# Dealing the mixing in two parts of nine steps per pair of heads, and scoring tiles 3 and 4 last

## The chip, the cores and the metric

The kernel runs on one core of a Trainium2 chip. The metric is device time in microseconds of one execution; the median of three runs of the kernel before is 802.76 us (802.55 to 803.49).

## What is computed

A windowed causal attention with a linear distance bias, for 8 batches of 8 heads, 576 positions and 64 channels a head; its output, as 576 rows of 512 channels per batch, goes through a gated mixing over the positions and a channel layer.

```python
scores = scale * np.matmul(q, k.transpose(0, 1, 3, 2))
mask = (rel >= 0) & (rel < window)                 # window = 128
scores = np.where(mask, scores + bias[None], -1000000000.0)
attn = np.exp(scores - np.max(scores, axis=-1, keepdims=True))
attn = attn / (np.sum(attn, axis=-1, keepdims=True) + 1e-09)
x = np.matmul(attn, v)                             # then heads side by side
theta = x @ w_theta
y = einsum('ts,bsd->btd', w_tok_r, x * cos(theta)) + einsum('ts,bsd->btd', w_tok_i, x * sin(theta))
u = x + y
out = u + np.maximum(u @ w_ch, 0.0)
```

## The kernel before

Queries are cut into five tiles (`TILES`, four of 128 and one of 64), and each meets a window of up to 256 keys. Products that need more than one pass of precision are made of a high and a low part (`qh`, `ql`, `kh`, `kl`, and so on), three products for one.

Four kinds of work make up a batch:

- **Attention**, by pairs of heads, four pairs a batch (`attend`). `Pair.scores(tiles)` (L272) makes the scores of some tiles for both heads of a pair: per tile six products with a contraction over 64 rows, two at a time, one for each head (L289, `s_ps`), then a DVE instruction that adds the bias and finds the row's extreme (L296), then an exponential on ACT (L300). The calls are (0, 2), (3, 4) and (1,), and belong to the *next* pair, one pair ahead. `flip` (in `turned`, L320) transposes a head's weights into `t_ps`; ACT copies them to fp16 (L366), DVE makes the low part (L367); `values` (L337) multiplies them with the values into `acc`, 27 products a head; `finish` (L343 to L346) scales and writes `x_sb`.
- **Turning** (`turn`): the batch's `x_sb` is transposed (L390), multiplied with `w_theta` (L410), and its sine and cosine are taken on ACT (L431, L432) and multiplied in (DVE, and L381, L382 for the split into `z_hi` and `z_lo`).
- **Mixing** (`mix`): 8 groups of 27 products (L469), each group in its own PSUM tile `mm`. One *step* of the generator is three products, so a group has nine steps and a batch 72. A group ends with L474 (DVE), L475 (ACT), L476 (POOL).
- **Channels** (`channels`, L489): 8 groups of 12 products, then L492 and an output DMA (L494).

While a batch is mixed, the next batch's attention runs: `attend` draws steps of the mixing (`other`) between its own calls. The sine and the exponential need different tables on ACT, so the exponentials of the scores are held behind the batch's last sine (`behind`).

The written order is not the order on the engines. The framework's scheduler orders the instructions on each engine by a priority that follows the written order, and by when it reckons each one ready; mixing, channels and turning carry an offset on that priority (`MIX`, `CHAN`, `ROTATE`). So a step that is written in one place can stand somewhere else on PE.

Other names: `prepare` (L175 to L234) splits a pair's q and k and issues the load of the next pair (DMAs from SP, L176, L178); `measure` (L201) is a DVE reduction over a group of four heads of values `vb`, which a DMA (L192) brings; `spread_scales` (L209 to L221) turns its result into scales; `ready` (L248 to L250) splits a head's values.

Of the kernel before, what the change touches and what calls it, by code (L numbers as in the profile page):

```python
# [29 lines left out]
DEPTH = 1  # L30
# [16 lines left out]
def attn_moe_kernel(ctx: ExitStack, tc: tile.TileContext, qt, kt, vx, wth, wtok, wch, band, out):  # L47
# [125 lines left out]
    def load_pair(p):  # L173
        b, h = divmod(2 * p, H)
        qr = ld.tile([128, S], F32, name="qr")  # L175
        nc.sync.dma_start(out=qr, in_=qt[b, h:h + 2].rearrange("h d s -> (h d) s"))  # L176
        kr = ld.tile([128, S], F32, name="kr")
        nc.sync.dma_start(out=kr, in_=kt[b, h:h + 2].rearrange("h d s -> (h d) s"))  # L178
        return qr, kr
# [15 lines left out]
    def measure(g):  # L195

        vb = group_v[g]
        most = rings["most"].take()  # L200
        nc.vector.tensor_reduce(out=most, in_=vb[:, :, :, :64], axis=mybir.AxisListType.XY, op=ALU.max,  # L201
                                apply_absolute_value=True)
        nc.vector.tensor_scalar(out=most, in0=most, scalar1=2.0 ** -100, scalar2=None, op0=ALU.max)
        group_v[g] = vb, most
# [20 lines left out]
    def split_pair(p, raw):  # L225

        qr, kr = raw
        qh, ql, kh, kl = (qk.tile([128, S], F32R, name=name) for name in ("qh", "ql", "kh", "kl"))
        sc = scales[:, p % (H // 2):p % (H // 2) + 1]
        nc.scalar.activation(qh, qr, AF.Copy, scale=sc)  # L230
        nc.vector.scalar_tensor_tensor(out=ql, in0=qr, scalar=sc, in1=qh.bitcast(F32), op0=ALU.mult,  # L231
                                       op1=ALU.subtract)
        nc.scalar.copy(kh, kr)  # L233
        nc.gpsimd.tensor_tensor(out=kl, in0=kr, in1=kh.bitcast(F32), op=ALU.subtract)  # L234
        return (qh, kh), (ql, kh), (qh, kl)
# [265 lines left out]
    def prepare(p):  # L501

        if 0 <= p - 1 < pairs and p - 1 not in parts:
            parts[p - 1] = split_pair(p - 1, raw.pop(p - 1))
        if p < pairs and p not in raw:
            raw[p] = load_pair(p)

    def step(stream, k=1):
        for _ in range(k):
            next(stream, None)  # L510
# [11 lines left out]
    def attend(b, x_sb, other, first, behind):  # L522

        for g in range(H // 2):
            p = b * H // 2 + g
            one, two = first.pop(0).heads
            new = None
            if p + DEPTH < pairs:
                new = Pair(p + DEPTH)
                first.append(new)  # L530

            def scores(tiles):
                if new is not None:
                    new.scores(tiles, behind)

            one.flip(0)
            one.flip(1)
            scores((0, 2))
            step(other, 6)
            one.values(0)  # L540
            one.values(1)
            one.finish(x_sb)
            if new is not None:
                new.heads[0].ready()
            two.flip(0)
            two.flip(1)
            scores((3, 4))
            if p % 2 == 0 and p + 2 < pairs:
                measure(p // 2 + 1)
            step(other, 6)  # L550
            two.values(0)
            two.values(1)
            two.finish(x_sb)
            scores((1,))
            if p % 2 == 0 and p + 2 < pairs:
                spread_scales(p // 2 + 1)
            prepare(p + DEPTH + 2)
            if new is not None:
                new.heads[1].ready()
            step(other, 6)  # L560

    def start(x_sb, load):

# [48 lines left out]
    def ahead(prods, chans):  # L612

        for k, _ in enumerate(prods):
            if k in AHEAD:
                next(chans)
            yield

    def ahead0(prods, chans):

        rest = urgent(unpack(LATE, ((uf, "xtf"),)), LATE0)
        for k, _ in enumerate(prods):
            if k % 4 == 3:
                next(rest, None)
            yield
        yield from rest
        for _ in range(AHEAD0):
            next(chans)
            yield
# [25 lines left out]
    for b in range(B):  # L655
        chans = urgent(channels(b, st[b]), CHAN if b else CHAN0)
        mixing = urgent(mix(st[b]), MIX if b else MIX0)
        other = ahead(mixing, chans) if b else ahead0(mixing, chans)
        if b + 1 < B:
            x_sb = xp.tile([128, NT, DM], F32, name="x_sb")  # L660
            attend(b + 1, x_sb, other, first, st[b]["sin"])
        for _ in other:
            pass
        if b + 1 < B:
            if first:
                st[b + 1]["exp"] = first[-1].exp
            rotated(urgent(turn(x_sb, st[b + 1]), ROTATE), chans)
        for _ in chans:
            pass
# [47 lines left out]
```

## Time and profile before

| what | value |
|---|---|
| median of the runs | 802.76 us |
| the profiled execution's own time | 803.77 us |
| its span, first to last instruction | 802.0 us |
| granted TensorE clock, mean | 0.991 |
| DVE busy | 567.2 us (71%) |
| ACT busy | 481.8 us (60%) |
| POOL busy | 260.6 us (32%) |

The span has a start (weights are loaded and split, attention of batch 0, to about 105 us), a turn of batch 0 (to about 155 us), seven stages in which batch b is mixed while batch b+1 is attended and then turned, and a tail in which the last batch is mixed alone. Five of the seven stages repeat with a period near 86.8 us. Busy time of PE includes matmuls that overlap, so it is read with the starts of the instructions, which the timeline gives.

### The profile page before, as it was taken

How to read it: one execution, taken by the hardware profiler on the slowest of the kernel's cores; microseconds unless marked ns; L12 is line 12 of the kernel's file. 1: busy time of each engine (PE TensorE's matmuls, PEld its weight loads, DVE VectorE, ACT ScalarE, POOL GpSimd, SP SyncE). 2: the span in 40 equal slices, each digit the busy share in tenths (PEclk: the TensorE clock that was granted, in tenths of full speed). 3: DMA queues.
4: the chain of work that ended last, by engine and by line, in shares of the span. 5: the costliest groups of instructions: out<-in, count | busy, mean ns of one | idle time of the engine just before them, and what ended most of it. 6: DMA issues, size and time to landing. Idle time of an engine off the chain costs nothing.

```text
span 802.0 us, 16393 instructions
## 1 busy us (share of the span) xinstructions
PE 740.5 (92%) x6338; PEld 656.0 (82%) x6338; DVE 567.2 (71%) x1535; ACT 481.8 (60%) x962; POOL 260.6 (32%) x324
## 2 busy tenths in 40 slices
PE   3565996889999999999999999999999999999998
PEld 2454875778788898889889988999888988899897
DVE  6997449877866877677767786687858776664712
ACT  5544347576567656775667657865767566844610
POOL 3576005552232322432252214232333225210530
PEclk9999999799999999999999999999999999999999
DMA  6541121132110221022112212023102211000001
GB/s 236 173 152 60 34 90 42 42 90 65 45 60 22 72 87 53 31 65 64 55 62 68 65 45 60 23 67 99 45 30 65 64 57 64 2 1 31 30 1 60
DMA packets 29549, 49.65 MB, mean 62 GB/s; under 512 B 2592, under 2 KB 19104, under 8 KB 29472
## 3 DMA queue, kind: packets, MB, share of 16 engines
q1 hardware_dynamic: 29472, 48.61, 19.3%
q8 instruction: 50, 0.82, 0.4%
q14 instruction: 27, 0.22, 0.1%
HBM read 39.16 MB, written 9.44 MB: 61 GB/s over the span
## 4 chain that ended last, share of the span: by engine, by line
PE 60%; DVE 16%; ACT 15%; issue 4%; DMA 3%; POOL 1%; SPq 0%; ACTq 0%; DVEq 0%; POOLq 0%
PE mm L469 19%; PE mm L489 10%; PE mm L410 8%; PE t_ps L320 8%; PE s_ps L289 7%; PE acc L337 7%; ACT s_sb L300 5%; DVE f L425 2%; DVE s_sb L296 2%; ACT z_hi L381 2%; ACT g L431 2%; PE mm L390 2%; DVE pt L367 1%; DMA vb<-in_vx_dram 1%; ACT L431 1%
## 5 line engine op out<-in xcount | busy, mean ns | idle before, releaser
L469 PE MATMUL mm<-wtk_hi,z_hi 128*128 128x288 f32 x576 | 172.8, 305 | 0.3 <-DVE xtf L474 0.3
L469 PE MATMUL mm<-wtk_lo,z_hi 128*128 128x288 f32 x576 | 172.0, 303 | 0.0
L469 PE MATMUL mm<-wtk_hi,z_lo 128*128 128x288 f32 x576 | 167.4, 301 | 0.0
L300 ACT ACTIVATE s_sb<-s_sb,fixed 128x256 f32<-128x256 f32 (+2 forms) x320 | 128.2, 465 | 56.5 <-DVE fixed L296 56.4
L296 DVE CUSTOM_DVE_ANT_0 s_sb<-s_ps,fixed 128x256 f32<-128x256 f32 (+2 forms) x320 | 105.5, 375 | 26.3 <-PE t_ps L320 12.7
L320 PE MATMUL t_ps<-fixed,s_sb 128*128 128x128 f32 (+1 forms) x576 | 104.0, 295 | 9.9 <-ACT s_sb L300 8.3
L469 PEld LDWEIGHTS mm<-wtk_hi,z_hi 128*128 128x128 f32 x576 | 108.8, 190 | 3.4 <-DVE xtf L474 0.5
L469 PEld LDWEIGHTS mm<-wtk_lo,z_hi 128*128 128x128 f32 x576 | 109.0, 190 | 2.0
L469 PEld LDWEIGHTS mm<-wtk_hi,z_lo 128*128 128x128 f32 x576 | 107.3, 190 | 0.9
L476 POOL TENSOR_TENSOR u_lo<-xtf,u_hi 128x288 fp32r<-128x288 f32 x64 | 52.6, 828 | 139.5 <-ACT u_hi L475 131.8
L367 DVE SCALAR_TENSOR_TENSOR pt<-t_ps,pt 128x512 f16<-128x512 f32 x112 | 74.8, 683 | 24.1 <-ACT pt L366 24.1
L382 POOL TENSOR_TENSOR z_lo<-g,z_hi 128x512 fp32r<-128x512 f32 x40 | 55.3, 1382 | 111.5 <-ACT z_hi L381 111.5
L320 PEld LDWEIGHTS t_ps<-fixed,s_sb 128*128 128x128 f32 (+1 forms) x576 | 67.4, 150 | 27.5 <-ACT s_sb L300 12.3
L289 PE MATMUL s_ps<-kh,qh 64*128 64x256 f32 (+2 forms) x320 | 57.5, 343 | 26.8 <-DVE fixed L296 19.8
L366 ACT ACTIVATE pt<-t_ps 128x512 f16<-128x512 f32 x112 | 63.3, 594 | 24.4 <-PE t_ps L320 23.9
L234 POOL TENSOR_TENSOR kl<-kr,kh 128x576 fp32r<-128x576 f32 x32 | 46.9, 1465 | 74.1 <-ACT kh L233 64.7
L289 PEld LDWEIGHTS s_ps<-kh,qh 64*128 64x128 f32 (+1 forms) x320 | 33.1, 192 | 41.7 <-DVE fixed L296 19.1
L337 PE MATMUL acc<-vh,pt 128*128 128x65 f16 x1008 | 61.2, 195 | 2.9 <-DVE pt L367 1.7
L337 PEld LDWEIGHTS <-pt 128*128 128x128 f16 x1512 | 52.8, 98 | 10.1 <-DVE pt L367 2.9
L289 PE MATMUL s_ps<-kh,ql 64*128 64x256 f32 (+2 forms) x320 | 50.8, 302 | 5.8 <-DVE ql L231 5.8
L337 PE MATMUL acc<-vl,pt 128*128 128x64 f16 x504 | 55.8, 193 | 0.0
L475 ACT CAST u_hi<-xtf 128x288 fp32r<-128x288 f32 x64 | 27.0, 430 | 44.5 <-DVE xtf L474 44.5
(111 smaller groups left out, 1570.0 us busy)
## 6 DMA issues: line engine op xcount, KB each, us to landing
vb<-in_vx_dram SPq DMA_DIRECT2D x16, 650.0 KB, 4.2
qr<-in_qt_dram SPq DMA_DIRECT2D x32, 288.0 KB, 3.1
kr<-in_kt_dram SPq DMA_DIRECT2D x32, 288.0 KB, 2.8
out_dram<-xtf SPq DMA_DIRECT2D x64, 144.0 KB, 1.8
xtf<-in_wtok_dram SPq DMA_DIRECT2D x4, 576.0 KB, 5.7
xtf<-in_wch_dram SPq DMA_DIRECT2D x4, 512.0 KB, 3.9
u_hi<-in_wtok_dram SPq DMA_DIRECT2D x3, 576.0 KB, 3.9
u_lo<-in_wtok_dram SPq DMA_DIRECT2D x2, 576.0 KB, 4.3
```

The costliest lines, as they stand in the source:

```text
L289: nc.tensor.matmul(ps[:qn, e, 256 * k:256 * k + kn], qm[rows, q0:q0 + qn], km[rows, k0:k0 + kn], start=(j == 0), stop=(j == len(self.terms ...
L296: nc.vector.tensor_tensor_reduce(out=sb, in0=ps[:qn, e, 256 * k:256 * k + kn], in1=bnd[:qn, c0:c0 + kn], scale=2.0 ** -((2 * self.p + e) % ...
L300: self.exp = nc.scalar.activation(sb, sb, AF.Exp, bias=least, scale=-1.0)
L320: nc.tensor.transpose(t_ps[:, off:off + w], self.sc[i][:, 128 * j:128 * j + 128], ident[:w, :w])
L337: nc.tensor.matmul(av[:, i, :r.shape[-1]], l, r, start=(n == 0), stop=(n == len(prods) - 1))
L366: nc.scalar.activation(pt[:, 0], t_ps, AF.Copy, scale=2.0 ** PEXP)
L367: nc.vector.scalar_tensor_tensor(out=pt[:, 1], in0=t_ps, scalar=2.0 ** PEXP, in1=pt[:, 0], op0=ALU.mult, op1=ALU.subtract)
L382: nc.gpsimd.tensor_tensor(out=z_lo[:, c, :], in0=z, in1=z_hi[:, c, :].bitcast(F32), op=ALU.subtract)
L410: nc.tensor.matmul(t_ps, a[:, c * 128:c * 128 + 128], w[:, c, :], start=(k == 0 and c == 0), stop=(k == len(prods) - 1 and c == 3))
L469: nc.tensor.matmul(y_ps[:, :HALF], z[:, c, m * 128:m * 128 + 128], w[:, c, cs], start=(k == 0), stop=(k == 26))
L476: nc.gpsimd.tensor_tensor(out=u_lo[:, m, cs], in0=xtf[:, m, cs], in1=u_hi[:, m, cs].bitcast(F32), op=ALU.subtract)
L489: nc.tensor.matmul(o_ps[:, :HALF], w[:, c, e * 128:e * 128 + 128], u[:, c, cs], start=(k == 0), stop=(k == 11))
```

## The change

Per pair of heads, the mixing was drawn in three parts of six steps; now it is drawn in two parts of nine, which is one group of 27 products each. The scores of tile 1 come before those of tiles 3 and 4 instead of after them, the second head's flips come ahead of them and of `ready` of the first head, `prepare` comes earlier (ahead of the scores of tiles 3 and 4), and the part of the mixing that closed the pair's turn is gone.

```diff
             scores((0, 2))
-            step(other, 6)
+            step(other, 9)
             one.values(0)
             one.values(1)
             one.finish(x_sb)
+            two.flip(0)
+            two.flip(1)
+            scores((1,))
             if new is not None:
                 new.heads[0].ready()
-            two.flip(0)
-            two.flip(1)
-            scores((3, 4))
             if p % 2 == 0 and p + 2 < pairs:
                 measure(p // 2 + 1)
-            step(other, 6)
+            prepare(p + DEPTH + 2)
+            scores((3, 4))
+            step(other, 9)
             two.values(0)
             two.values(1)
             two.finish(x_sb)
-            scores((1,))
             if p % 2 == 0 and p + 2 < pairs:
                 spread_scales(p // 2 + 1)
-            prepare(p + DEPTH + 2)
             if new is not None:
                 new.heads[1].ready()
-            step(other, 6)
```

The scheduler's order moves with it on every engine. On PE, before, in a stage of the repeating kind where the next pair's tiles 0 and 2 are scored among the mixing, these rows stand together (`s_ps` holds scores, `mm` a mixing group):

```order
L469 MATMUL mm<-wtk_hi,z_hi 128x288
L289 MATMUL s_ps<-kh,ql 64x192 x2
L289 MATMUL s_ps<-kl,qh 64x192 x2
L289 MATMUL s_ps<-kh,qh 128x256 x2
L289 MATMUL s_ps<-kh,ql 128x256 x2
L289 MATMUL s_ps<-kl,qh 128x256 x2
L469 MATMUL mm<-wtk_lo,z_hi 128x288
```

On PE now, in every second stage of the repeating kind, where tiles 0 and 2 are first scored among the mixing, the rows are (`acc` is the output of a head, `pt` its turned weights):

```order
L289 MATMUL s_ps<-kh,qh 64x192 x2
L289 MATMUL s_ps<-kh,ql 64x192 x2
L289 MATMUL s_ps<-kl,qh 64x192
L469 MATMUL mm<-wtk_hi,z_lo 128x288 x3
L337 LDWEIGHTS pt
L337 MATMUL acc<-vh,pt 128x65
L337 LDWEIGHTS pt
L337 MATMUL acc<-vl,pt 128x64
L289 MATMUL s_ps<-kl,qh 64x192
L289 MATMUL s_ps<-kh,qh 128x256 x2
L289 MATMUL s_ps<-kh,ql 128x256
```

The twelve score products are cut into more runs, with mixing and value products between them, and two of the cuts fall between the two heads of a pair of products (the rows without "x2").

On DVE, before, ahead of the first `measure` (L201) of a stage of the repeating kind, after the `vl` that last reads the old values:

```order
L250 SCALAR_TENSOR_TENSOR vl<-vb,fixed,vh 128x320
L367 SCALAR_TENSOR_TENSOR pt<-t_ps,pt 128x512 x2
L296 ISA s_sb_4134,fixed<-s_ps,fixed 128x128
L296 ISA fixed 128x1
L296 ISA s_sb_4135,fixed<-s_ps,fixed 128x128
L296 ISA fixed 128x1
L474 TENSOR_TENSOR xtf<-mm,xtf 128x288 x3
L231 SCALAR_TENSOR_TENSOR ql<-qr,fixed,qh 128x576
L201 TENSOR_REDUCE fixed<-vb 128x4
```

On DVE now, at the same place:

```order
L250 SCALAR_TENSOR_TENSOR vl<-vb,fixed,vh 128x320
L367 SCALAR_TENSOR_TENSOR pt<-t_ps,pt 128x512 x2
L474 TENSOR_TENSOR xtf<-mm,xtf 128x288 x3
L201 TENSOR_REDUCE fixed<-vb 128x4
L343 TENSOR_SCALAR fixed<-acc,fixed 128x5
L250 SCALAR_TENSOR_TENSOR vl<-vb,fixed,vh 128x320
L203 TENSOR_SCALAR fixed<-fixed 128x4
L367 SCALAR_TENSOR_TENSOR pt<-t_ps,pt 128x512
```

The two L296 and the `ql` no longer stand between the release of the old values and the reduction over the new ones.

## Prediction

> **What bounds the kernel now.** I began with the page, for the share of each engine and the slices.
>
> ```profile
> span 802.0 us, 16393 instructions
> PE 740.5 (92%) x6338; PEld 656.0 (82%) x6338; DVE 567.2 (71%) x1535; ACT 481.8 (60%) x962; POOL 260.6 (32%) x324
> PE   3565996889999999999999999999999999999998
> PEclk9999999799999999999999999999999999999999
> PE 60%; DVE 16%; ACT 15%; issue 4%; DMA 3%; POOL 1%; SPq 0%; ACTq 0%; DVEq 0%; POOLq 0%
> ```
>
> PE is busy nearly everywhere after the sixth slice, at full clock. The chain that ended last lies on PE for 60% of the span; DVE and ACT hold 31%, so they still decide some pieces. Then the windows, by stage: columns are length, busy time of PE, PEld, DVE, ACT and POOL with counts, granted clock, DMA share and GB/s.
>
> ```profile
> 105.00:155.00 50.00, 40.06 (x244) 32.40 (x244) 39.54 (x90) 29.18 (x53) 20.91 (x18) 0.93 0.23 69
> 155.00:249.70 94.70, 88.03 (x792) 78.17 (x793) 71.50 (x192) 61.06 (x122) 31.42 (x41) 0.96 0.19 59
> 423.60:510.40 86.80, 86.25 (x805) 77.10 (x804) 64.65 (x187) 58.07 (x117) 26.24 (x37) 1.00 0.19 58
> 683.90:756.20 72.30, 71.20 (x641) 64.36 (x640) 43.15 (x114) 44.01 (x91) 18.00 (x23) 1.00 0.04 13
> ```
>
> The row in the middle, 423.60:510.40, stands for the five stages that repeat. PE idles 86.80 - 86.25 = 0.55 us there: no engine's wait is left worth removing, and the number of products doesn't change. What can still change is how long PE takes for them, since their order changes. The first mixing stage is different: PE idles 94.70 - 88.03 = 6.67 us, waiting mostly for DVE (its waits come below).
>
> **What a score run costs PE.** The third view is PE's timeline in the repeating stage. The first column is the start; I read starts alone, since the ends of matmuls are modelled.
>
> ```profile
> 439.21 0.29 PE L469 MATMUL mm<-wtk_hi,z_lo 128*128 128x288 f32 x1
> 439.34 0.29 PE L469 MATMUL mm<-wtk_hi,z_hi 128*128 128x288 f32 x1
> 439.57 0.30 PE L289 MATMUL s_ps<-kh,ql 64*64 64x192 f32 x2
> 439.71 0.26 PE L289 MATMUL s_ps<-kl,qh 64*64 64x192 f32 x2
> 439.79 0.31 PE L289 MATMUL s_ps<-kh,qh 64*128 64x256 f32 x2
> 439.94 0.28 PE L289 MATMUL s_ps<-kh,ql 64*128 64x256 f32 x2
> 440.05 0.28 PE L289 MATMUL s_ps<-kl,qh 64*128 64x256 f32 x2
> 440.27 0.40 PE L469 MATMUL mm<-wtk_lo,z_hi 128*128 128x288 f32 x1
> 440.51 0.29 PE L469 MATMUL mm<-wtk_hi,z_lo 128*128 128x288 f32 x1
> ...
> 442.58 0.30 PE L469 MATMUL mm<-wtk_hi,z_hi 128*128 128x288 f32 x1
> 442.72 0.60 PE L320 MATMUL t_ps<-fixed,s_sb 128*128 128x128 f32 x4
> 443.07 0.38 PE L469 MATMUL mm<-wtk_lo,z_hi 128*128 128x288 f32 x1
> 443.29 0.29 PE L469 MATMUL mm<-wtk_hi,z_lo 128*128 128x288 f32 x1
> ```
>
> Mixing products follow each other every 0.13 us (439.21 to 439.34), and pairs of score products every 0.08 to 0.15 us, 0.12 in the mean. From the mixing product at 439.34 to the second one behind the scores, at 440.51, is 1.17 us. Two mixing products (0.26) and five pairs (0.60) make 0.86, so the run of scores has cost **0.31 us** beyond its products: 0.23 instead of 0.13 on entering, 0.22 and 0.24 on leaving. Full-height transposes don't: 442.58 to 443.29 is 0.71 us, and two mixing products and four transposes at some 0.11 are 0.70. So it is the change between 64-row and 128-row products that costs, whatever the number of products in a run.
>
> **The change part by part.** *Score runs.* I counted in PE's order how often score products stand in a run, with other work on both sides: 133 runs in the whole program before, 158 now. By stage of mixing, from the first: 16, 15, 17, 17, 17, 17, 8 before and 18, 19, 23, 21, 23, 21, 7 now; the start and the tail don't change. That is 25 more, at 0.31 us each 7.75 us. The bounds for one run are 0 (it lies where PE would have waited) and 0.40, nearly what a run costs when its product and weight loads also arrive late; I take 0.31, the row. The two extra runs of the first mixing stage I count as nothing, 0.62 less, since PE waits 6.67 us there anyway. Left: **+7.1**.
>
> *Pairs cut in two.* Some of the new cuts fall between the two heads' products of a pair, as in the second piece of the order. I count 25 of them beyond the few of before. Two products that start together take one spacing of 0.12; apart, each could take its own. Bounds 0 and 25 x 0.12 = 3.0; the rows show no cut pair, so I take the middle less a little, **+1.2**.
>
> The Trainium skill (TensorE: Matmul & The Clock Gate, Part 3: Packing small matmuls) says that products in different row groups start some 4 ns apart and run at once, but that products start and end in program order; by that a cut pair would lose the whole overlap, an estimate of 3.0 rather than 1.2 and a sum higher by 1.8. The rows of "x2" above agree with the overlap; what a cut pair costs no row quoted here shows.
>
> *Mixing steps.* The same 216 products stand in the stage, and "whole groups" isn't what PE gets: the order now has runs of mixing up to 42 products long and still cuts groups at 24, because the mixing's priority lets it fill in. A cut beside transposes costs nothing (the row at 442.72), so: 0.
>
> *The wait for the low part of `pt`.* The one wait of PE over 0.2 us in the repeating stage, from PE's timeline, and behind it rows of the chain of waits and of the groups by line in that stage:
>
> ```profile
> 433.34 0.20 PE L337 MATMUL acc<-vl,pt 128*128 128x64 f16 x1
> 433.76 0.24 PE L337 MATMUL acc<-vh,pt 128*128 128x65 f16 x2 [0.23 <-DVE pt L367]
> ...
> 423.62 1.28 ACT L300
> 424.91 5.12 ACT s_sb L300 x14
> ...
> L367 DVE SCALAR_TENSOR_TENSOR pt<-t_ps,pt 128x512 f16<-128x512 f32 x16 | 10.8, 684 | 3.4 <-ACT pt L366 3.4
> L366 ACT ACTIVATE pt<-t_ps 128x512 f16<-128x512 f32 x16 | 9.1, 595 | 3.6 <-PE t_ps L320 3.6
> ```
>
> The value products wait from 433.34 to 433.76 (0.42, instead of some 0.03), because ACT first had 14 held exponentials behind the table load, 1.28 + 5.12 us. Now 15 or 16 stand there, 0.4 to 0.8 us more; but PE has 5 to 6 us of work between these transposes and their value products, where it had 3.6. So this wait goes: -0.39 in each of five stages, **-2.0**. What is late next: later in the stage there are value products that follow their transposes after only 1.4 to 1.7 us of PE work, where the shortest before was 2.7 (the products that stand between in PE's order, each at its spacing in the timeline). ACT's copy and DVE's low part take 0.595 + 0.684 = 1.28 in a row, so 1.4 is just enough with empty queues and not enough with a score reduction ahead. Bounds per stage 0 and 2; I take 0.4, near the 0.39 of the row: **+2.0**.
>
> *`measure` and the values' DMA.* In the second piece of the order, DVE's reduction moves ahead, past two L296 and a `ql`. The transfer sets when it can start (rows of the waits, of the tile `vb`, and of DVE's timeline):
>
> ```profile
> DVE fixed L201 <- DMA vb<-in_vx_dram: 1.4, 1, 1.4
> DMA to landing us min/median/max: 4.1/4.1/4.2
> 436.52 1.49 DVE L201 TENSOR_REDUCE fixed<-vb 128x4 f32<-128x1280 f32 x1
> 435.74 0.85 DVE L231 SCALAR_TENSOR_TENSOR ql<-qr,fixed,qh 128x576 fp32r<-128x576 f32 x1
> 434.22 0.28 DVE L296 CUSTOM_DVE_ANT_0 s_sb<-s_ps,fixed 128x128 f32<-128x128 f32 x1
> ```
>
> The first reduction starts at 436.52 with DVE busy until then; without 0.85 and twice 0.21 (the spacing of the two L296 is below their 0.28) it is reached 1.2 us earlier, while the 4.1 us of the transfer don't shrink. DVE then stands for about that, and behind it in its queue are `finish`, a `vl`, and the low part that the next head's value products wait for. PE has some 24 to 30 mixing products (at 0.13, over 3 us) to do meanwhile, so I cost it at 0; if that cover were gone it is 1.2 a stage, six stages, 7 us.
>
> *`prepare` earlier.* Its q and k loads on SP pass the values' load and some output DMAs, and its `kl` on POOL stands ahead of a split of z. Before, SP's loads of k wait for buffers, not PE for loads:
>
> ```profile
> SPq L178 <- POOL kl L234: 194.2, 24, 15.9
> ```
>
> This is 194 us of waiting in 24 issues that nobody waited for; one `kl` ahead of the last `z_lo` could cost a POOL instruction, but ACT's exponentials stand in front of that z anyway. 0, with bounds -1 and +1.5 a stage at one place.
>
> *First mixing stage.* Here PE waits for DVE:
>
> ```profile
> PE s_ps L289 <- DVE fixed L296: 5.8, 3, 2.8
> PE mm L216 <- DVE fixed L213: 1.5, 1, 1.5
> ```
>
> The new order has one more score group ahead of the second of these waits, and six mixing products in front of the first score group behind it; both fill waiting, 0.5 us or so each: **-1.0**, with bounds -5 and +3, as DVE's work is the same and only its order moves.
>
> **The sum.** 7.1 + 1.2 - 2.0 + 2.0 - 1.0 = **+7.3 us**. The profiled execution took 803.77 us, so 811.1; the median of the runs is 1.0 below it, and on that scale the forecast is **810.1 us**.
>
> **The rivals.**
>
> *Faster, by the first stages.* If the new runs lie mostly where PE would otherwise wait, a run costs a tenth of a us, 2.5 in all, and a DVE order that lets PE through takes 5 of the 6.67 us of the first mixing stage and the 2.0 of the `pt` waits: 2.5 - 5 - 2.0 = -4.5, 798.3 us. It decides from the point where the stage 155 to 250 shrinks by more than the repeating stages grow. For it: only there is idle time to win, and PE's waits for score reductions before 172 us alone were 5.8 us. Against it: 0.55 us of idle time a repeating stage can't hide four to six new runs (1.2 to 1.9 us). Chance 0.18.
>
> *Nothing comes of it.* The runs are hidden or the scheduler has traded them for waits of the same size; the sum is between -1.6 and +1.6, 802.8. That the groups of 27 don't stand whole on PE speaks for it, the count of runs against it. Chance 0.14.
>
> *Waits take the stage.* The close value products wait a full score reduction and a low part more, twice a stage, 2 x 0.7 to 2 x 1.0, and `measure` stops DVE without cover: some 8 us on top, 818 us. Against it: DVE idles a quarter of the stage (64.65 of 86.80 busy). Chance 0.14.
>
> **How the numbers follow.** My forecast, more runs of scores with about the same waits, has 0.54. Slower by over 0.2% (1.6 us, what a measurement here can tell from no change) is the forecast and the waits, 0.68; same 0.14; faster 0.18. The range 800 to 817 leaves out the better part of the faster rival and the far side of the waits, some 0.2.
>
> **What would show it.** In the changed kernel's windows the repeating stages should come out 0.8 to 2 us longer each, in pairs of two kinds (the order alternates), with PE still idle under 1.5 us; the stage before 250 us should be equal or up to 1.5 us shorter. PE's timeline at the second piece of the order should show an extra 0.2 to 0.3 us at each cut. The wait at the first value products behind the exponentials should be gone. I am wrong if the repeating stages keep 86.8 us with 21 or 23 runs of scores, or if PE's idle time grows by more than the runs cost.

## The result, and the profile after

The changed kernel takes 820.72 us (median of 4 runs, 819.51 to 821.96), against 803.12 us (802.55 to 803.89) for the kernel before on the same chip: a ratio of 1.0219, 95% interval 1.0200 to 1.0237, or **+17.6 us**. The forecast was 810.1 us in a range of 800 to 817. The sign was right, and the size was not: it is more than twice what the sum gave, and outside the range.

First the page of the changed kernel, the lines that answer to those of before:

```profile
span 817.7 us, 16414 instructions
PE 754.9 (92%) x6338; PEld 660.3 (81%) x6338; DVE 570.4 (70%) x1535; ACT 483.1 (59%) x962; POOL 263.7 (32%) x324
PE   3566997799999999999999999999999999999998
PE 63%; DVE 20%; ACT 10%; issue 4%; DMA 2%; POOL 1%; SPq 0%; DVEq 0%; ACTq 0%; POOLq 0%
```

As many matmuls as before, 14.4 us more PE time and 3.2 us more DVE time. The share of DVE on the chain that ended last rose from 16% to 20%, while ACT's fell. That is the first hint that more than PE's order is at stake, and it says nothing of the place.

The place comes from cutting a stage at ACT's table loads. From the load of the exponential's table to the load of the sine's, the stage is mostly attention and mixing; from the sine's to the exponential's it is the turn. These are the windows of two stages of the kernel before (length, busy time of PE, PEld, DVE, ACT and POOL with counts, clock, DMA share, GB/s):

```profile
336.80:399.00 62.20, 61.10 (x637) 54.65 (x636) 47.16 (x153) 41.39 (x90) 14.29 (x29) 1.00 0.19 56
399.00:423.60 24.60, 24.51 (x165) 21.72 (x164) 17.45 (x35) 16.70 (x28) 11.93 (x9) 1.00 0.19 60
423.60:485.80 62.20, 61.73 (x642) 55.38 (x641) 47.22 (x153) 41.41 (x90) 14.35 (x29) 1.00 0.19 57
485.80:510.40 24.60, 24.51 (x165) 21.73 (x164) 17.43 (x35) 16.66 (x28) 11.89 (x9) 1.00 0.20 61
```

And the same two stages of the changed kernel:

```profile
337.20:399.80 62.60, 61.94 (x625) 54.49 (x623) 43.07 (x140) 39.57 (x86) 11.97 (x27) 1.00 0.20 58
399.80:428.60 28.80, 27.70 (x183) 23.51 (x183) 22.22 (x48) 19.07 (x32) 14.44 (x10) 1.00 0.17 49
428.60:491.20 62.60, 61.66 (x628) 54.63 (x627) 43.05 (x140) 39.20 (x85) 12.44 (x27) 1.00 0.19 57
491.20:518.80 27.60, 26.60 (x175) 22.70 (x174) 23.16 (x47) 18.92 (x33) 14.92 (x10) 1.00 0.16 50
```

A stage, an attention part and the turn behind it, went from 86.8 us to 91.4 and 90.2 us, and nearly all of it lies in the turn: 24.6 us became 28.8 and 27.6. Over the five repeating stages, cut in the same way, it is 19.3 us, all but 1.7 of it in the turns. DVE has 12 to 13 instructions and about 5 us more in the turn, and 4 us less in the attention; 10 to 18 matmuls moved the same way. The attention part lost that work and did not get shorter: 62.2 became 62.6 us. PE now idles 1.0 to 1.1 us in a turn, where it idled 0.1.

What PE waits for in the repeating stages is the next view, the table of PE's waits (total us, times, longest), first of the kernel before and then of the changed one:

```profile
PE acc L337 <- DVE pt L367: 1.4, 5, 0.5
PE t_ps L320 <- ACT s_sb L300: 1.1, 3, 0.4
PE mm L489 <- ACT xtf L403: 0.8, 4, 0.2
```

```profile
PE s_ps L289 <- DVE ql L231: 4.8, 5, 1.4
PE t_ps L320 <- ACT s_sb L300: 2.9, 6, 0.7
PE mm L410 <- DVE f L425: 0.9, 2, 0.4
```

The wait of the value products for `pt` is gone, as forecast. In its place stands one wait in each of the five stages for **`ql`**, the low part of q that `prepare` makes on DVE. PE's timeline shows one of them, in a turn of the changed kernel (start, length, and in brackets the idle time and what ended it):

```profile
496.91 0.30 PE L289 MATMUL s_ps<-kh,qh 64*64 64x192 f32 x2
498.21 0.31 PE L289 MATMUL s_ps<-kh,ql 64*64 64x192 f32 x2 [1.00 <-DVE ql L231]
498.36 0.26 PE L289 MATMUL s_ps<-kl,qh 64*64 64x192 f32 x2
```

PE has issued the products with `qh`, reaches those with `ql`, and stops 1 us in the middle of a score group. DVE's timeline at that place shows why `ql` is late:

```profile
494.94 1.47 DVE L436 TENSOR_TENSOR f<-x_sb,f 128x512 f32<-128x512 f32 x1
496.32 1.84 DVE L231 SCALAR_TENSOR_TENSOR ql<-qr,fixed,qh 128x576 fp32r<-128x576 f32 x1
498.08 0.68 DVE L425 SCALAR_TENSOR_TENSOR f<-f,mm 128x512 f32<-128x512 f32 x1
```

and POOL's, beside it:

```profile
494.42 1.43 POOL L234 TENSOR_TENSOR kl<-kr,kh 128x576 fp32r<-128x576 f32 x1 [8.34 <-ACT kh L233]
495.81 1.73 POOL L382 TENSOR_TENSOR z_lo<-g,z_hi 128x512 fp32r<-128x512 f32 x1
497.51 1.79 POOL L382 TENSOR_TENSOR z_lo<-f,z_hi 128x512 fp32r<-128x512 f32 x1
```

`ql` stands in DVE's queue behind the product of L436, and both take twice their time: with POOL idle beside them, L436 takes 0.69 and `ql` 0.80 (at 517.45 in the same trace), here 1.47 and 1.84. POOL's `kl` and `z_lo` run at the same moment, and the DVE instruction ends some 0.6 us after POOL's does (498.16 against 497.54).

The other `ql` of the turn stands at its end. This is the chain of waits of the changed kernel at the end of the first of the two turns and into the next stage (start, us, what; rows of "issue" of up to 0.04 us left out):

```profile
423.50 1.47 DVE f L425
424.97 2.00 DVE ql L231
426.97 0.35 DVE g L427
427.34 0.72 ACT g L431
428.06 0.52 ACT f L432
428.60 1.28 ACT L300
429.90 3.39 ACT s_sb L300 x9
433.33 0.44 PE t_ps L320 x2
```

The last tile's angle (L425, then L427), the sine and cosine, the table load and the held exponentials follow each other, and a `ql` of 2.00 us has come between the two DVE instructions. Before, L427 started 0.03 us behind L425's end here.

The new cuts look as forecast. This is PE's timeline in the changed kernel at the second piece of the order, where the two halves of a pair stand apart:

```profile
346.46 0.25 PE L289 MATMUL s_ps<-kl,qh 64*64 64x192 f32 x1
346.63 0.66 PE L469 MATMUL mm<-wtk_hi,z_lo 128*128 128x288 f32 x3
347.13 0.20 PE L337 MATMUL acc<-vh,pt 128*128 128x65 f16 x1
347.18 0.20 PE L337 MATMUL acc<-vl,pt 128*128 128x64 f16 x1
347.30 0.30 PE L289 MATMUL s_ps<-kl,qh 64*64 64x192 f32 x1
347.30 0.44 PE L289 MATMUL s_ps<-kh,qh 64*128 64x256 f32 x2
```

From the last score to the mixing it is 0.17 us, where a pair of scores takes 0.12; the three mixing products take 0.50 instead of 0.39; and from the last value product back to the scores it is 0.12, where value products take some 0.04. That is 0.24 us for the cut, in the 0.2 to 0.3 that was forecast. The second half of the cut pair starts together with a product of the next pair, at 347.30, so it doesn't take a spacing of its own.

### The profile page after: what moved, and what is told of

The parts are those of the page before. It is cut to its first block, busy times and chain, and to the rows that moved or that the text cites. A ratio compares the mean times of both kernels' runs of the same rounds, so it can differ in the third digit from the quotient of the medians.

```text
span 817.7 us, 16414 instructions
## 1 busy us (share of the span) xinstructions
PE 754.9 (92%) x6338; PEld 660.3 (81%) x6338; DVE 570.4 (70%) x1535; ACT 483.1 (59%) x962; POOL 263.7 (32%) x324
## 4 chain that ended last, share of the span: by engine, by line
PE 63%; DVE 20%; ACT 10%; issue 4%; DMA 2%; POOL 1%; SPq 0%; DVEq 0%; ACTq 0%; POOLq 0%
PE mm L469 23%; PE t_ps L320 9%; PE mm L489 8%; PE acc L337 8%; PE s_ps L289 7%; PE mm L410 5%; DVE f L425 3%; DVE s_sb L296 3%; DVE ql L231 2%; ACT s_sb L300 2%; DVE g L427 2%; ACT g L431 2%; PE mm L390 2%; DVE g L434 1%; DVE f L436 1%
## 5 line engine op out<-in xcount | busy, mean ns | idle before, releaser
L469 PE MATMUL mm<-wtk_hi,z_lo 128*128 128x288 f32 x576 | 169.7, 302 | 0.6 <-POOL z_lo L382 0.6
L296 DVE CUSTOM_DVE_ANT_0 s_sb<-s_ps,fixed 128x256 f32<-128x256 f32 (+2 forms) x320 | 105.5, 374 | 37.2 <-PE s_ps L289 23.2
L320 PE MATMUL t_ps<-fixed,s_sb 128*128 128x128 f32 (+1 forms) x576 | 104.9, 296 | 12.4 <-ACT s_sb L300 11.8
L366 ACT ACTIVATE pt<-t_ps 128x512 f16<-128x512 f32 x112 | 62.8, 591 | 26.2 <-PE t_ps L320 25.5
L234 POOL TENSOR_TENSOR kl<-kr,kh 128x576 fp32r<-128x576 f32 x32 | 49.4, 1542 | 85.7 <-ACT kh L233 78.3
L289 PE MATMUL s_ps<-kh,qh 64*128 64x256 f32 (+2 forms) x320 | 58.7, 347 | 19.0 <-DVE fixed L296 12.0
L289 PE MATMUL s_ps<-kh,ql 64*128 64x256 f32 (+2 forms) x320 | 52.7, 306 | 11.4 <-DVE ql L231 11.4
L431 ACT ACTIVATE g<-g,fixed 128x512 f32<-128x512 f32 (+1 forms) x40 | 29.0, 724 | 53.3 <-DVE g L427 52.9
```

The lines of the kernel that those rows point to most:

```text
L289: nc.tensor.matmul(ps[:qn, e, 256 * k:256 * k + kn], qm[rows, q0:q0 + qn], km[rows, k0:k0 + kn], start=(j == 0), stop=(j == len(self.terms ...
L296: nc.vector.tensor_tensor_reduce(out=sb, in0=ps[:qn, e, 256 * k:256 * k + kn], in1=bnd[:qn, c0:c0 + kn], scale=2.0 ** -((2 * self.p + e) % ...
L320: nc.tensor.transpose(t_ps[:, off:off + w], self.sc[i][:, 128 * j:128 * j + 128], ident[:w, :w])
L366: nc.scalar.activation(pt[:, 0], t_ps, AF.Copy, scale=2.0 ** PEXP)
L469: nc.tensor.matmul(y_ps[:, :HALF], z[:, c, m * 128:m * 128 + 128], w[:, c, cs], start=(k == 0), stop=(k == 26))
```

## The experiments

The expectations speak of theories by name. **Runs**: the loss is the 25 more runs of 64-row score products, at 0.31 us each. **Turn**: it is the score work and q and k splits that moved into the turn, where DVE and ACT decide. **Place**: it is the new position of `prepare`. Later: **q split**, the `ql` on DVE in the turn, against **reductions**, the score reductions (L296) that came there with it. Each kernel's result is a median and its ratio to the kernel before, with the 95% interval. "Score runs" are counted in PE's order of that kernel: 133 before, 158 in the changed kernel. How they are counted matters a little: if every other product ends a run, also the transposes over 64 rows, the traces have 140 and 162.

### One part of the change at a time

`prepare` back at its old place, all else changed:

```diff
             if p % 2 == 0 and p + 2 < pairs:
                 measure(p // 2 + 1)
-            prepare(p + DEPTH + 2)
             scores((3, 4))
...
                 spread_scales(p // 2 + 1)
+            prepare(p + DEPTH + 2)
```

> The changed kernel with prepare written at its old place, behind spread_scales; all else as changed. Three theories. RUNS: the changed kernel is slower because its score products stand in more runs on PE (158 against 133), at 0.31 us each. TURN: it is slower because more score work of the next pair (score products, their DVE reductions, the q split ql and the POOL split kl) lies between the batch's first sine and the next table load for the exponentials, where DVE and ACT form the chain: 10 reductions and 2 ql in those stretches instead of 6 and 1. PLACE: it is slower because prepare comes earlier and its q split collides. The order of this kernel has the same 158 runs and the same 10 reductions as the changed one. RUNS and TURN: 820 to 822 us, same as the changed kernel. PLACE: 806 to 812 us.

Measured: 822.01 us, 1.0227 (1.0211 to 1.0242). The written place of `prepare` is no cause. It is what Runs and Turn gave (820 to 822), and not what Place gave. The scheduler gives nearly the same order from both places (158 score runs again), and PE waits the same 4.8 us for `ql`.

The two parts of nine alone, in the kernel before (the changed kernel with the calls between `step(other, 9)` back in the old order):

```diff
-            step(other, 6)
+            step(other, 9)
...
-            step(other, 6)
+            step(other, 9)
...
-            step(other, 6)
```

> The kernel before with the dealing alone changed: 9 and 9 steps, no third part; scores, flips and prepare as before. In its order: 153 runs of scores (before 133), 10 reductions in the turn instead of 6, one ql. RUNS: 20 more runs at 0.31 us, 809 us. TURN: the extra reductions lengthen each turn by 2.5 us or so, six turns, some 815 to 818 us.

Measured: 814.24 us, 1.0130 (1.0114 to 1.0145), with 153 runs. That is above Runs (809) and just under Turn (815 to 818); PE has no wait for `ql`.

The scores of tile 1 and of tiles 3 and 4 exchanged, in the kernel before, with 6/6/6 kept:

```diff
-            scores((3, 4))
+            scores((1,))
...
-            scores((1,))
+            scores((3, 4))
```

> The kernel before with the scores of tile 1 and of tiles 3 and 4 exchanged; dealing 6, 6, 6, prepare as before. In its order: 145 runs; the turns alternate between 6 and 12 reductions. RUNS: 12 more runs, 807 us, with the longer stages where the runs are (a no-wait sum 2.2 us higher in the stages that hold 6 reductions). TURN: three turns of 12 reductions, 3 to 3.6 us each, 812 to 814 us, with the turns alternating in length by that much.

Measured: 812.28 us, 1.0101 (1.0084 to 1.0118), with 145 runs, in the range of Turn (812 to 814). The turns alternate as Turn said, 24.8 and 29.8 us. But by ACT's table loads the attention in front of them alternates the other way, 65.1 and 58.7 us, so that the stages come out at 89.9 and 88.5 us, the shorter with the longer turn. **A long turn is no loss by itself**: work that stands in it is missing in the attention. In the changed kernel the turn is longer and the attention isn't shorter.

The changed kernel with the mixing dealt in 6/6/6 again:

```diff
-            step(other, 9)
+            step(other, 6)
...
-            step(other, 9)
+            step(other, 6)
...
+            step(other, 6)
```

> The changed kernel with the dealing back at 6, 6, 6; scores, flips and prepare as changed. In its order: 148 runs; the turns alternate between 6 and 10 reductions, and the stages with 6 hold more runs. RUNS: 15 more runs, 808 us. TURN: three turns of 10, 2.5 us each, 810 to 811 us, the turns alternating by 2 to 3 us. If the dealing itself is the cause: 803 to 804 us.

Measured: 815.54 us, 1.0156 (1.0128 to 1.0184), with 148 runs, above what any theory gave. So the dealing alone costs 10.4 us, everything but the dealing 12.5, the exchange of the scores alone 8.1, and the whole change 17.6: the parts don't add up. In this kernel the turns alternate: 27.6 us where two `ql` stand in the turn, 25.4 us where there is one, and PE's waits for `ql` are 4.2 us in three stages.

### The price of a run

In the kernel before, one extra product in front of each of the 64 mixing groups, into unused columns of the group's PSUM tile; nothing reads it. One kernel contracts over 64 rows, the other over 128; PE's order is the same row for row.

```diff
                 y_ps = ps_m.tile([128, 512], F32, name="mm")
+                nc.tensor.matmul(y_ps[:, 320:384], z_hi[:64, 0, :128], wtk_hi[:64, 0, :64], start=True, stop=True)
```

> The kernel before with one small extra product ahead of each of the 64 mixing groups, into columns that nothing reads, contracting over 64 rows (128x64 out). Its order on PE is the same, row for row, as that of the kernel with 128 rows in its place. RUNS: each extra product is a run of 64-row work among 128-row work and costs 0.31 us beyond itself, so this kernel is 64 x 0.31 = 20 us slower than the one with 128 rows (15 to 22, since some lie in waits). TURN: the two take the same time within 2 us.

> The same extra product over 128 rows. RUNS and TURN: 64 products at 0.1 us or less, 4 to 8 us over before, 807 to 812 us, changed order included.

Measured: 819.07 us (1.0187, 1.0170 to 1.0204) over 64 rows, and 805.60 us (1.0027, 1.0016 to 1.0038) over 128. The 64-row product and its return cost 13.5 us in 64 places, **0.21 us a run**; Runs gave 20 (15 to 22), Turn none. The extra product itself, by the trace of the first and then of the second kernel (duration min/median/max, then what its engine sat idle for):

```profile
L466 PE MATMUL mm<-wtk_hi,z_hi x64: 190/294/419, 143.9 to 794.1; 64*128 64x64 f32 x64
  issue: 7.7, 46
```

```profile
L466 PE MATMUL mm<-wtk_hi,z_hi x64: 191/193/298, 144.3 to 779.7; 128*128 128x64 f32 x64
```

A product of the same width takes 0.10 us more over half the rows, and PE stands still ahead of it for 7.7 us in 46 places, put down to "issue", that is, to nothing that the trace shows of another engine. The price of a run is real, and here a third cheaper than the 0.31 us of the prediction. It is the price of one product over half the rows alone; that a run of score products, in pairs over both halves, costs the same is taken over from it and not measured.

### Fewer runs by force

The score products of one call as a unit that nothing may enter, in both kernels:

```diff
+            with tc.tile_critical():
                 for k, i in enumerate(tiles):
```

> The kernel before with the products of one call of scores kept together (a critical section of the scheduler), so that no other PE work comes between them: 96 runs instead of 133, all whole. RUNS: 37 runs less, 11 us below before, 792 to 795 us, if no new waits come. TURN: its turns hold 6 reductions and one ql as before: 803 to 805 us. If PE has to stand while a call's last operands are not ready: 806 us or more, with PE waiting at the first score product.

> The changed kernel with the products of one call of scores kept together in the same way: 96 runs instead of 158. RUNS alone: 19 us below the changed kernel, 801 to 803 us. Runs and the ql's waits together: the turns hold 2 to 6 reductions and one or two ql, so part of the waits stays, 804 to 809 us. TURN alone: 810 to 815 us.

Measured: 927.10 us (1.1546, 1.1512 to 1.1581) for the kernel before and 944.84 us (1.1768, 1.1719 to 1.1817) for the changed one. This tells nothing of runs, since the unit itself waits:

```profile
L290 PE MATMUL s_ps<-kh,qh 64*128 64x256 f32 (+2 forms) x320 | 56.2, 347 | 125.9 <-DMA kr<-in_kt_dram 28.1
```

PE sat idle 125.9 us ahead of the first products of these units, where it waits until everything that the unit needs is there.

A gentler way is a higher priority for the score products, in the changed kernel:

```diff
+            with tc.high_priority(300):
                 for k, i in enumerate(tiles):
```

> The changed kernel with its score products, and nothing else, at a higher priority. In its order 115 runs of scores (before 133, changed 158), none cut between two heads, and 2 reductions and one ql in the turn. RUNS: 18 fewer than before, 5 us below it at best, 799 to 802 us. TURN: as before or a little less, 801 to 803 us. If the dealing in nines by itself leaves PE short of mixing products where value products wait: 808 us or more, with the waits in the attention stretches.

Measured: 805.59 us, 1.0021 (1.0012 to 1.0031), with 115 runs, repeating turns of 24.9 to 25.4 us and no wait for `ql`. It takes back 15 of the 17.6 us, less than Runs (799 to 802) and Turn (801 to 803) gave, and changes runs and waits together.

### Work moved out of the turn, or added to it

`prepare` of a stage's first pair held behind DVE's last product of the turn, in the changed kernel and in the kernel before:

```diff
-            prepare(p + DEPTH + 2)
+            with tc.issue_after(hold.ins) if g == 0 else nullcontext():
+                prepare(p + DEPTH + 2)
```

> The changed kernel with one edge more: the q split of the first pair of a batch's attention is held on DVE behind the last product of the turn before it. In its order no ql lies in the turn and 4 reductions instead of 10, but the runs of scores rise to 165 (before 133, changed 158). RUNS (0.31 us for each run of score products): 32 more runs than before, 814 us or, with the waits of the changed kernel kept, 822 to 825 us. TURN (score work and q split in the stretch between the sines and the exponentials): the turns come back to 24.6 us and the kernel to 806 to 809 us. A mixture, runs and the ql's waits each for about half: 813 to 817 us, with the turn's waits gone and the attention stretches longer.

> The kernel before with the same edge. In its order no ql in the turn, 2 reductions instead of 6, 140 runs of scores instead of 133. RUNS: 2 to 4 us longer than before, 806 to 808 us. TURN: the turns get shorter by 0.5 to 1 us each, 799 to 802 us.

Measured: 816.52 us (1.0155, 1.0131 to 1.0180) for the changed kernel and 808.69 us (1.0060, 1.0045 to 1.0075) for the kernel before. The first is what the mixture gave (813 to 817). In the changed kernel the turns fall to 24.2 to 25.4 us without a `ql`, and PE's waits for `ql` from 4.8 to 0.3 us; the attention grows from some 62.6 to 64.7 us and more. It takes back 5 us although it has 7 runs more. In the kernel before, where nothing waited for `ql`, the hold only does harm: the turns get shorter, to 22.8 to 23.8 us, as Turn said, and the attention grows from some 62.2 to 65.5.

Two extra DVE products of 64 partitions by 512, which nothing reads, at the last angle of each turn, in the kernel before:

```diff
+            if i == 0:
+                for _ in range(2):
+                    nc.vector.tensor_tensor(out=spare[:64], in0=f[:64], in1=x_sb[:64, 0, :], op=ALU.mult)
```

> The kernel before with two more DVE products per batch, 64x512 each, at the last angle of the turn (their result is not used). By the order the first of them stands between that angle's two steps, the second behind them, and the runs of scores fall to 126 from 133. RUNS: 2 us less than before, 801 to 802 us. TURN: 0.7 to 1.4 us more for each of seven turns that something waits for, 808 to 812 us.

Measured: 804.16 us, 1.0014 (1.0005 to 1.0024), with 126 runs, and not the 808 to 812 of Turn. The repeating turns grow by only 0.4 to 0.6 us. More DVE time at the turn's end costs little by itself, which speaks for the second `ql`, at the end of the chain above, as the smaller harm, and for the one in the middle, for which score products stand waiting on PE, as the larger. That is argued; no run takes away one of the two alone.

### The low part of q taken off DVE

Most experiments so far moved `ql` and the score reductions together. These four kernels part them. In the first two, `ql` isn't made at all and the products take `qh` in its place; the output is then not the reference's, and PE has as many products.

```diff
-        nc.vector.scalar_tensor_tensor(out=ql, in0=qr, scalar=sc, in1=qh.bitcast(F32), op0=ALU.mult,
-                                       op1=ALU.subtract)
...
-        return (qh, kh), (ql, kh), (qh, kl)
+        return (qh, kh), (qh, kh), (qh, kl)
```

> The kernel before without the low part of q: the products of ql with kh take qh in its place (so as many products, and the scores are not the reference's), and DVE's 32 instructions of L231 are left out. PE's order has 127 runs of scores, and 6 reductions stand between the first product with the angle's multiple and the last in each turn, as before. RUNS: 6 runs fewer than before, 801 to 803 us. Q SPLIT (the waits come from ql on DVE in the turn): little here, since before has one ql in a turn at no great wait: 798 to 802. REDUCTIONS (the waits come from the score reductions that stand in the turn): as many as before, 800 to 803. It is the base for the next kernel.

> The changed kernel without the low part of q, likewise. PE's order has 130 runs of scores, 3 more than its base, and 34 cut pairs instead of 14, but 12 reductions stand in each turn where the base has 6 (10 in the first), and no ql in either. Difference to the base: RUNS: 3 x 0.21 to 0.31, +1 at most, with the cut pairs +3. Q SPLIT: 0 beyond that, -2 to +3. REDUCTIONS: 34 reductions more in six turns, at 0.21 to 0.4 us of DVE each 7 to 14 us, +7 to +14.

Measured: 795.52 us (0.9907, 0.9890 to 0.9925) and 798.10 us (0.9929, 0.9912 to 0.9946). **Without the q split on DVE the change costs some 2 us**, and the two intervals overlap. The first is faster than any theory gave: even in the kernel before, where PE waited for no `ql` in the repeating stages, leaving it out saves 7.5 us. These are two turns of each, the first kernel ahead. Counted between ACT's table loads, the first kernel has 4 reductions in each and the second 11 and 10, where the kernel before has 4 and the changed kernel 10:

```profile
301.90:326.20 24.30, 24.30 (x160) 21.14 (x160) 16.75 (x34) 16.62 (x29) 10.98 (x9) 1.00 0.18 55
388.40:413.20 24.80, 24.80 (x163) 21.57 (x163) 17.87 (x35) 16.99 (x30) 11.10 (x9) 1.00 0.15 54
```

```profile
298.10:323.80 25.70, 25.70 (x170) 22.21 (x170) 21.18 (x52) 17.73 (x31) 12.26 (x11) 1.00 0.16 54
385.20:411.90 26.70, 26.70 (x176) 22.97 (x176) 21.22 (x49) 18.28 (x31) 12.05 (x11) 1.00 0.16 55
```

In the second kernel DVE is nearly as busy as in the changed kernel's turns, 21.2 us, and PE doesn't idle: the turns are longer because PE has 10 and 13 more products in them, and the attention has become shorter for it, from some 62.1 us to some 61. Reductions, which gave +7 to +14, are refuted.

With a `ql` of 32 columns instead of 576, which no product reads (so again another output), DVE's instruction stays in its queue with its wait for ACT:

```diff
-        nc.vector.scalar_tensor_tensor(out=ql, in0=qr, scalar=sc, in1=qh.bitcast(F32), op0=ALU.mult,
+        nc.vector.scalar_tensor_tensor(out=ql[:, :32], in0=qr[:, :32], scalar=sc, in1=qh[:, :32].bitcast(F32), op0=ALU.mult,
```

> The kernel before with the low part of q made for 32 of 576 columns only, read by no product (qh in its place, as in q1): DVE's instruction stays where it stands and keeps its wait for ACT's qh, but is short. 124 runs of scores, 5 to 6 reductions and one short ql in a turn. RUNS: 9 runs fewer than before, 800 to 802. Q SPLIT and REDUCTIONS: 798 to 803. Base for the next kernel.

> The changed kernel with the short low part of q, likewise: 129 runs of scores, 12 reductions and one or two short ql in a turn. Difference to the base: RUNS: 5 x 0.21 to 0.31, +1.6 at most. Q SPLIT by its DVE time: 0; by its wait for ACT's qh alone: +3 to +6. REDUCTIONS: some 39 more in six turns, +7 to +14.

Measured: 798.73 us (0.9941, 0.9927 to 0.9956) and 804.13 us (1.0005, 0.9995 to 1.0015). Here the change costs 5.1 us by the ratios, in the range given for the wait of `ql` on ACT's `qh` alone. PE's waits in this pair's second kernel are for `pt` (1.9 us) and for DVE's `xtf` (1.8 us), and for no `ql`; what makes these late stays open.

The last pair computes all, with `ql` on POOL:

```diff
-        nc.scalar.activation(qh, qr, AF.Copy, scale=sc)
-        nc.vector.scalar_tensor_tensor(out=ql, in0=qr, scalar=sc, in1=qh.bitcast(F32), op0=ALU.mult,
-                                       op1=ALU.subtract)
+        nc.scalar.activation(qr, qr, AF.Copy, scale=sc)
+        nc.scalar.copy(qh, qr)
+        nc.gpsimd.tensor_tensor(out=ql, in0=qr, in1=qh.bitcast(F32), op=ALU.subtract)
```

> The kernel before with the low part of q made on POOL in place of DVE (ACT scales q in place first, one ACT instruction more a pair). PE's order has 156 runs of scores instead of 133, and 10 reductions in most turns, with no ql on DVE in any. RUNS: 23 more at 0.21 to 0.31, 808 to 811. Q SPLIT ON DVE: the runs' price less up to 7 us (what taking the ql away saved in the kernel before): 801 to 805. REDUCTIONS alone: was refuted by the pair without ql.

> The changed kernel with the low part of q on POOL, likewise. 143 runs of scores instead of 158, 12 reductions in the turns, no ql on DVE. RUNS: 15 fewer, 815 to 818. Q SPLIT ON DVE: turn waits of 7 us gone as well, 806 to 811, unless POOL, where kl and z_lo stand in the turn too, becomes the engine that is waited for there: then 815 to 822.

Measured: 814.31 us (1.0126, 1.0101 to 1.0151) and 811.15 us (1.0100, 1.0069 to 1.0131). The changed kernel gains 9.6 us by the move, more than Runs gave (815 to 818) and at the upper end of what the q split gave (806 to 811), and PE waits for no `ql`; its turns have 12 reductions, and the two at 308 and 396 us last 26.2 and 27.1 us with PE busy throughout. The kernel before loses 10 us by the ratio, more than any theory gave; its order has 23 more runs, and the rest isn't accounted for. So this pair says little of the change itself. None of the kernels that compute the reference's output beats the one before.

### The rearranged kernels side by side

Time lost is the ratio less one, times 803 us; "rest" is what is left after 0.21 us for each run more or fewer than 133. The last column is PE's waits for `ql` in the repeating stages, from the view of PE's waits.

| kernel | lost, us | runs | rest, us | waits for `ql`, us |
|---|---|---|---|---|
| the changed kernel | 17.6 | 158 | 12.3 | 4.8 |
| `prepare` back | 18.2 | 158 | 13.0 | 4.8 |
| changed, 6/6/6 | 12.5 | 148 | 9.4 | 4.2 |
| 9/9 alone | 10.4 | 153 | 6.2 | 0 |
| scores exchanged alone | 8.1 | 145 | 5.6 | 0 |
| changed, first `prepare` held | 12.4 | 165 | 5.7 | 0.3 |
| before, first `prepare` held | 4.8 | 140 | 3.3 | 0 |
| changed, score priority | 1.7 | 115 | 5.5 | 0 |
| changed, `ql` on POOL | 8.0 | 143 | 5.9 | 0 |
| before, `ql` on POOL | 10.1 | 156 | 5.3 | 0 |
| before, two DVE products more | 1.1 | 126 | 2.6 | 0 |

The three kernels in which PE waits 4 us or more for `ql` are the three with the largest rest. All others in the table lose 3 to 6 us beyond their runs. The four kernels with no `ql` or a short one have less to do and so aren't in it; reckoned alike, their rests are -6.2 (before) and -5.1 (changed) without `ql`, and -2.8 and 1.2 with the short one.

## Why the prediction was right or wrong

*Score runs, +7.1.* Right in kind, and too large in price. The count of 25 stood, and the price of 0.31 us, read from one place of the timeline, was 0.21 where it was measured: 5.3 us for all 25, or 4.8 for the 23 that the sum counts. So the sign was right for a reason that held, and the larger part of the loss came from elsewhere.

*Cut pairs, +1.2.* Not measured by itself. The higher estimate of 3.0 us that the prediction gives beside it doesn't fit the trace. Where the second half of a cut pair goes on into further score products, it starts within 4 ns of the next one, as at 347.30, in all 12 such places from 250 us on. Where it stands apart from other scores, it is a run of its own, which the first term has priced already.

*The wait for `pt`, -2.0.* Right in kind: the row, 1.4 us in five places, is gone from PE's waits. *Close value products, +2.0*: no such wait is among the three shown for the changed kernel; it didn't come. *`measure`, 0*: its reduction now waits longer for the values' DMA, but PE has no wait behind it in that table, so the cover held.

*First mixing stage, -1.0.* Too small, on the right side and within its bounds. The exponential's table load that ends it came at 249.71 us before and comes at 246.92 us now.

*`prepare`, 0.* For the written place of `prepare` this stood: with it back at the old place the kernel takes 822.01 us.

*The premise that the waits stay about the same.* **This is the step that failed.** "PE idles 0.55 us" was taken to mean that only PE's order could change the time, and for the turn this was a statement about one order only. The prediction weighed the loads on SP and `kl` on POOL, and left out the instruction that `prepare` has on DVE: `ql`, which the score products of the next pair wait for. It read DVE over the whole stage and not over the turn. In the new order, ten reductions and two `ql` stand in a stretch that had four reductions, one `ql` and 17 us of DVE work in all, beside the angle products and beside POOL's splits. By the profile, PE waits 4.8 us for `ql` in the five repeating stages and 1.8 us more than before for the exponentials (the `t_ps` row). An estimate from the starts of PE's products alone (the median spacing of each kind of neighbours, summed over each order) says that of the 19.3 us some 8.5 are the new order where nothing waits, and 10 to 11 are waits, 7 to 9 of them in the turns; it shifts by some 2 us with how the neighbours are sorted.

So of the 17.6 us, 5.3 go with the runs at the measured price, and 12.3 are left. Some 7 of these go with the `ql` in the turn: that is what the rest falls by when `prepare` is held out of the turn (12.3 to 5.7), and what parts the changed kernel from those with no wait for `ql`. The other 5 or so aren't explained by one mechanism. They are no fixed price of rearranging either, since without `ql` the same change costs some 2 us in all. That pair shows that the loss hangs on `ql` on DVE. It can't show by which path: taking `ql` away also changes the scheduler's order, to 127 and 130 runs instead of 133 and 158, so the extra runs go with it.

*The rivals.* "Waits take the stage", with 0.14, came nearest in time, 818 us, but named the value products and `measure`; the waits that came were others. Its argument against, that DVE idles a quarter of the stage, is a mean over the stage: in the turn of the changed kernel DVE is busy 22.22 of 28.80 and 23.16 of 27.60 us, and the chain of waits at its end runs over DVE and ACT. The prediction's own mark, repeating stages 0.8 to 2 us longer with PE idle under 1.5 us, was missed: they were 4.6 and 3.4 us longer, with PE idle for 1.8 and 1.9 us.

## What to carry to other kernels

When a step is moved, list what it issues on *every* engine and who waits for each piece, and read each engine's load in the stretch where the piece lands, not over the stage. An engine that idles a quarter of a stage can be what PE waits for in its busiest third. A stretch that grows is a loss only if the others don't shrink by as much, so the whole stage is read as well. A bound that holds in one order ("PE never waits") says nothing of the next, so the order on DVE and POOL is read for the whole of the stretch that received work, not only at the places where the diff cuts.

## What the hardware showed

A product over 64 rows between products over 128 rows cost 0.21 us beyond the same product over 128 (819.07 against 805.60 us, 64 places). Of the 8.7 us for which PE stood still ahead of it, the trace names another engine for 1.0.

DVE instructions with two operands in SBUF often stretched beyond the end of a POOL instruction that ran when they started: `ql` to 1.84 and 2.07 us from 0.80, L436 to 1.47 from 0.69. L427, with one operand, stretched as well, from 0.42 to as much as 1.54 us. L425 with one of its operands in PSUM (`mm`) didn't: 0.67 to 0.69 us in all 21 cases beside POOL. In the turn's end, from DVE's timeline and then POOL's:

```profile
423.50 1.47 DVE L425 SCALAR_TENSOR_TENSOR f<-g,f 64x512 f32<-64x512 f32 x1
424.90 2.07 DVE L231 SCALAR_TENSOR_TENSOR ql<-qr,fixed,qh 128x576 fp32r<-128x576 f32 x1
```

```profile
423.13 1.29 POOL L382 TENSOR_TENSOR z_lo<-f,z_hi 128x512 fp32r<-128x512 f32 x1
424.38 1.98 POOL L234 TENSOR_TENSOR kl<-kr,kh 128x576 fp32r<-128x576 f32 x1
```

POOL's two end at 424.42 and 426.36, and DVE's two end 0.55 and 0.61 us after. The Trainium skill (SBUF — State Buffer, SBUF: two separate sides) calls the pair of ports that DVE and GpSimd share an exclusive lock, held for a whole instruction, which a DVE instruction with two SBUF inputs needs as well; these rows agree. POOL pays too: `kl`, started at 424.38, takes 1.98 us and `z_lo` at 497.51 1.79, where `z_lo` at 423.13 takes 1.29. In the kernel before, an L436 at 406.81 kept its 0.68 us, and the `z_lo` beside it took 1.99. So the length of `ql` depends on what POOL does beside it, and the 0.85 us that the prediction read for it in the attention couldn't stand for the turn.
